# Queries and keys of the last batch: block-wise loads and a VectorE block transpose instead of TensorE transposes

## The chip, the core and the metric

The kernel runs on one core of a Trainium2 chip. The metric is the device time of one execution in microseconds (us). The core has five engines that run their own instruction queues in order and meet through semaphores: TensorE (PE; its weight loads are listed apart as PEld), VectorE (DVE), ScalarE (ACT), GpSimd (POOL) and SyncE (SP, which issues nearly all DMAs here).

## What is computed

Three layers follow one another: attention in which 32 global tokens see everything and 512 local tokens see the global ones and a window of 32 to either side; a two-layer perceptron over all tokens; and a soft mixture of experts. All data are float32, the two perceptron weights come as float64. Batch is 4, heads 8, head size 64. Cut to what matters:

```python
def _attn_ref(q_l, k_l, v_l, q_g, k_g, v_g):
    scale = 1.0 / np.sqrt(D)                      # D = 64
    def sm(s):
        s = s - np.max(s, axis=-1, keepdims=True)
        e = np.exp(s)
        return e / (np.sum(e, axis=-1, keepdims=True) + 1e-09)
    s_g = scale * np.matmul(q_g, k_all.transpose(0, 1, 3, 2))
    out_g = np.matmul(sm(s_g), v_all)
    s_ll = scale * np.matmul(q_l, k_l.transpose(0, 1, 3, 2))
    s_ll = np.where(np.abs(pos[:, None] - pos[None, :]) <= 32, s_ll, -1000000000.0)
    s_lg = scale * np.matmul(q_l, k_g.transpose(0, 1, 3, 2))
    a_l = sm(np.concatenate([s_lg, s_ll], axis=-1))
    out_l = np.matmul(a_l, np.concatenate([v_g, v_l], axis=2))
    return np.concatenate([out_g, out_l], axis=2)

def _moe_ref(x, w_in, w_out):
    h = x @ w_in
    return np.maximum(0.01 * h, h) @ w_out

def _moe2_ref(x, phi, w1, w2):
    logits = x @ phi                              # 32 slots, 8 experts
    slot_input = softmax_over_tokens(logits).T @ x
    slot_out = relu(slot_input[e] @ w1[e]) @ w2[e]   # for each expert e
    return softmax_over_slots(logits) @ slot_out
```

## The kernel before

**Pairs of heads.** Attention is done for 16 pairs (batch b, two heads i), counted here n = 4b + i; pairs 12 to 15 are those of batch 3. One pair goes through these steps:

- `load_qk` (L157): keys `kn` and queries `qn` come from memory with the token on the partition, two DMAs of 128 KB per tensor, in runs of 256 bytes (one token of one head). Both tiles have two buffers.
- `a_T` (L383): four 128x128 transposes on PE per tensor (L390) into a PSUM bank of the tag "tp" (two banks), and an ACT copy (L394) to `kT` (four buffers) and `qT` (two); the queries are multiplied by the scale in that copy. DVE then lays out the windows `kw` (L405 the keys of the window, L406 the global keys; three buffers, two per pair).
- `a_S` (L418): 32 small score matmuls (L434) into two banks of the tag "sc" (two banks), one for each head; DVE adds the mask and takes the maximum (L446), negates it (L452, `nmx`), ACT takes the exponential (L454).
- `a_E` (L465): eight transposes of the exponentials (L473) and two DVE copies (L477, `eT`); `a_V` (L481): 32 matmuls with the values (L493) and the division by the sum (L501, `xn`).

Each L434 or L493 instruction of the program shows as two matmul records in the trace.

After a batch's four `a_T`, `g_S` (L508) does the scores of its global tokens: matmuls `gl` (L519) over all four `kT` of the batch, again in the two "sc" banks, maxima on DVE (L530 to L532, `gnmx`), exponentials on ACT (L536, L542). A `kT` buffer is free for the next batch when these matmuls are done, an "sc" bank when its exponential is.

**Beside it runs the perceptron** of earlier tokens: `b_H` (L674), 12 matmuls of 128x512 per quarter (L689) into one of two "hb" banks, which ACT empties (L696, `g`); DVE block transposes `g` (L708) into `gb`, POOL moves the blocks (L717); then the soft router: `lg` (L740, L755, L800), DVE and ACT softmax (L759 to L795, ACT L764, L769, L792), and `up` (L810), which takes an "hb" bank too and is added up by DVE (L815).

**What sets the order.** Items of both strands are merged by weights written in the code (`step`, `b_items`, `merge`), and the framework then orders each engine's queue by a timeline of its own. What an engine does next is therefore fixed in the program: an instruction whose data are late holds all that stand behind it on that engine. `last_a` names the newest attention matmul, after which a held perceptron item may be issued.

**Loads** for pair n+2 are issued on SP when `a_T` of pair n is written, values (`load_v`, L167) when `a_V` is; SP waits in its queue until the buffer is free. `load_vn` (L203) brings the values of a whole batch, 1 MB in one DMA.

Of the kernel before, what the change touches and what calls it, by code (L numbers as in the profile page):

```python
# [8 lines left out]
F32 = mybir.dt.float32  # L9
# [11 lines left out]
def kernel(  # L21
# [15 lines left out]
    nc = tc.nc  # L37
    B, H, S, D = q_l.shape
# [23 lines left out]
    def tp(name):  # L62
        return bank("tp", name, 2)
# [93 lines left out]
    def load_qk(b, i, ts=(None, None)):  # L157
        for src, nm, t in ((k_l, "kn", ts[0]), (q_l, "qn", ts[1])):
            if t is None:
                t = sa.tile([P, NT, 2, D], F32, tag=nm, name=nm, bufs=2)  # L160
            for h in range(2):
                nc.sync.dma_start(
                    out=t[:, :, h, :], in_=src[b, 2 * i + h].rearrange("(t p) d -> p t d", p=P)
                )
            nat[nm, b, i] = t
# [217 lines left out]
    def a_T(b, i):  # L383
        qn, kn = nat.pop(("qn", b, i)), nat.pop(("kn", b, i))
        for src, dst, nm, bf in ((kn, kT, "kT", 4), (qn, qT, "qT", 2)):
            pt = tp(nm + "p")
            if b == 0:
                warm(pt)
            for T in range(NT):
                last_a[0] = nc.tensor.transpose(  # L390
                    pt[:, P * T:P * T + P], src[:, T].rearrange("p h d -> p (h d)"), ident
                ).ins
            t = sa.tile([P, S], F32, tag=nm, name=nm, bufs=bf)
            nc.scalar.activation(  # L394
                out=t, in_=pt, func=AF.Copy, scale=scale if nm == "qT" else 1.0,
            )
            dst[b, i] = t
        kt = kT[b, i]
        HW = NW // 2
        kwin[b, i] = []  # L400
        for hf in range(2):
            kw = sa.tile([P, HW, P], F32, tag="kw", name="kw", bufs=3)
            src = kt[:, 32 * HW * hf:32 * HW * hf + 96]
            src = bass.AP(src.tensor, src.offset, [src.ap[0], [32, HW], [1, 96]])
            nc.vector.tensor_copy(kw[:, :, 0:96], src)  # L405
            nc.vector.tensor_copy(  # L406
                kw[:, :, 96:128],
                kgT[:, i, 32 * b:32 * b + 32].unsqueeze(1).to_broadcast([P, HW, 32]),
            )
            kwin[b, i].append(kw)  # L410
# [7 lines left out]
    def a_S(b, i):  # L418
# [3 lines left out]
        sm = sa.tile([P, NT, 2], F32, tag="sm", name="sm", bufs=2)  # L422
        rs = sa.tile([P, NT, 2], F32, tag="rs", name="rs", bufs=2)
        es = []
        bks = [bank("sc", f"sc{e}", 2) for e in range(2)]
        if b == 0:
            for bk in bks:
# [12 lines left out]
        for e in range(2):  # L440
            bk = bks[e]
            s = sa.tile([P, S + SG], F32, tag="se", name="se", bufs=4)[:, 0:S].rearrange(
                "p (t k) -> p t k", t=NT
            )
            for T in range(NT):
                nc.vector.tensor_tensor_reduce(  # L446
                    out=s[:, T, :], in0=bk[:, P * T:P * T + P],
                    in1=mask[:, 0 if T == 0 else 2 if T == NT - 1 else 1, :],
                    scale=1.0, scalar=-3.0e38, op0=ALU.add, op1=ALU.max,
                    accum_out=mx[:, e, T:T + 1],  # L450
                )
            nc.vector.tensor_scalar_mul(nmx[:, e], mx[:, e], -1.0)  # L452
            for T in range(NT):
                exp_last[0] = nc.scalar.activation(  # L454
                    out=s[:, T, :], in_=s[:, T, :], func=AF.Exp,
                    bias=nmx[:, e, T:T + 1], accum_out=sm[:, T, e:e + 1],
                ).ins
            es.append(s)
        nc.vector.tensor_scalar_add(sm, sm, 1e-9)
# [921 lines left out]
```

## Time and profile before

| | |
|---|---|
| median of 3 runs | 500.24 us (499.12 to 501.63) |
| profiled execution, its own time | 496.2 us |
| span of the profile | 494.5 us |
| PE busy | 463.5 us, 94% of the span |
| DVE, ACT, POOL busy | 56%, 47%, 32% |
| granted PE clock, mean | 0.979 of full speed |

All times of single instructions below come from the one profiled execution, whose span is 494.5 us. They are counted from the start of that span. Matmuls overlap, so what a group of them costs is read from its first start to the first start of the next group; the duration written beside it is longer. Batch 3 goes through attention between about 190 us (first load) and 325 us.

### The profile page before, as it was taken

The numbers are of one execution on the slowest core, as the hardware profiler recorded it, in microseconds if no ns is written. First come the engines' busy times: TensorE is split into PE (matmuls) and PEld (weight loads), VectorE is DVE, ScalarE is ACT, GpSimd is POOL, SyncE is SP. The second block draws the span as 40 slices with busy tenths as digits, with TensorE's granted clock in tenths as the row PEclk, the third lists the DMA queues.
The fourth block names the chain that finished last, engine by engine and source line by source line (L and its number), as shares of the span: only waits on it lengthen the run. The fifth ranks groups of instructions, "written<-read, shape, count | busy, mean of one in ns | idle before, by whom it ended". The sixth has DMA issues, their size and how long they took to land.

```text
span 494.5 us, 13438 instructions
## 1 busy us (share of the span) xinstructions
PE 463.5 (94%) x5323; PEld 322.0 (65%) x5323; DVE 275.0 (56%) x886; ACT 234.3 (47%) x680; POOL 160.3 (32%) x281
## 2 busy tenths in 40 slices
PE   7867889999989999999999999999999999999993
PEld 5645668666766657776777676777777777533463
DVE  4585888498547776556554656427666511413332
ACT  4776899588655345543435444234444432201122
POOL 2044887342400113460615243243667700000000
PEclk9986899999999999999999999999999999999998
DMA  9989598599457655334250231169420079999977
GB/s 177 223 200 267 183 292 313 185 304 311 150 143 144 143 118 93 85 76 129 60 106 1 60 60 45 44 220 405 150 78 2 23 266 357 364 397 371 305 237 214
DMA packets 118362, 90.23 MB, mean 182 GB/s; under 512 B 75356, under 2 KB 100764, under 8 KB 118300
## 3 DMA queue, kind: packets, MB, share of 16 engines
q1 hardware_dynamic: 115628, 88.33, 61.8%
q10 hardware_dynamic: 2672, 1.05, 0.8%
q8 instruction: 42, 0.69, 0.6%
q14 instruction: 20, 0.16, 0.1%
HBM read 76.68 MB, written 8.65 MB: 173 GB/s over the span
## 4 chain that ended last, share of the span: by engine, by line
PE 78%; DVE 4%; ACT 4%; DMA 1%; issue 1%; POOL 0%; ACTq 0%; DVEq 0%; POOLq 0%
PE hp L689 38%; PE gtp L726 4%; PE ehp L1221 3%; PE sc L434 3%; PE up L810 3%; PE po L493 3%; PE lg L740 2%; PE etp L473 2%; PE sop L1297 2%; PE sop L1275 1%; PE gpo L579 1%; PE wotp L345 1%; PE qTp L390 1%; PE kTp L390 1%; PE xtp L659 1%; PE gl L519 1%
## 5 line engine op out<-in xcount | busy, mean ns | idle before, releaser
L689 PE MATMUL hp<-wi,xxh 128*128 128x512 f32 x512 | 167.2, 408 | 1.2 <-ACT xxh L665 1.2
L689 PEld LDWEIGHTS hp<-wi,xxh 128*128 128x128 f32 x512 | 91.8, 190 | 28.2 <-issue 8.2
L717 POOL COPY g<-gb 32x256 f32<-32x256 f32 x206 | 82.7, 401 | 82.6 <-DVE gb L708 55.5
L689 PE MATMUL hp<-wi,xxl 128*128 128x512 f32 x256 | 101.0, 396 | 0.0
L696 ACT ACTIVATE g<-hp 128x512 f32<-128x512 f32 x60 | 35.3, 595 | 56.2 <-PE hp L689 54.2
L454 ACT ACTIVATE se<-se,nmx 128x128 f32<-128x128 f32 x128 | 49.6, 390 | 21.5 <-DVE nmx L452 21.4
L689 PEld LDWEIGHTS hp<-wi,xxl 128*128 128x128 f32 x256 | 48.3, 189 | 12.5 <-issue 1.7
L200 POOL COPY vw<-vw 32x1664 f32<-32x1664 f32 x10 | 15.8, 1575 | 78.3 <-DMA vw<-in_v_g_dram 34.9
L446 DVE CUSTOM_DVE_ANT_0 se<-sc,mask 128x128 f32<-128x128 f32 x128 | 28.9, 284 | 12.1 <-PE sc L434 12.0
L261 POOL TENSOR_TENSOR wn<-wn,rraw 128x512 int32<-128x512 int32 x16 | 22.8, 1435 | 34.5 <-DVE wn L257 33.0
L708 DVE STREAM_TRANSPOSE gb<-g 128x512 f32<-128x512 f32 x32 | 22.2, 702 | 19.3 <-ACT g L696 14.0
L434 PE MATMUL sc<-kw,qT 64*32 64x128 f32 x1024 | 29.2, 283 | 0.8 <-DVE mx L446 0.4
L493 PE MATMUL po<-vw,eT 128*32 128x64 f32 x1024 | 24.2, 232 | 3.5 <-issue 2.1
L261 POOL TENSOR_TENSOR wo<-wo,rraw 128x512 int32<-128x512 int32 x12 | 16.0, 1332 | 31.7 <-DVE wo L257 7.2
L434 PEld LDWEIGHTS sc<-kw,qT 64*32 64x32 f32 x1024 | 19.8, 109 | 8.9 <-issue 5.3
L493 PEld LDWEIGHTS po<-vw,eT 128*32 128x32 f32 x1024 | 18.4, 116 | 10.2 <-issue 7.4
L477 DVE COPY eT<-etp 128x512 f32<-128x512 f32 x28 | 18.7, 684 | 9.9 <-PE etp L473 9.9
L454 ACT ACTIVATION_READ_ACCUMULATOR se<-se,nmx 128x1 f32 x128 | 24.1, 188 | 0.0
L473 PE MATMUL etp<-identr,se 128*128 128x128 f32 x128 | 22.4, 296 | 0.2
L405 DVE COPY kw<-kT 128x672 f32<-128x672 f32 x32 | 19.8, 653 | 3.1 <-ACT kT L394 2.7
L251 ACT ACTIVATE rraw<-rraw 128x512 int32<-128x512 uint32 x28 | 18.7, 673 | 4.3 <-DMA rraw<-in_moe_w_out_dram 3.1
L473 PEld LDWEIGHTS etp<-identr,se 128*128 128x128 f32 x128 | 15.8, 146 | 6.3 <-ACT se L454 2.3
(232 smaller groups left out, 777.9 us busy)
## 6 DMA issues: line engine op xcount, KB each, us to landing
ew<-in_moe_w_dram SPq DMA_DIRECT2D x23, 1024.0 KB, 9.5
rraw<-in_moe_w_in_dram SPq DMA_DIRECT2D x16, 512.0 KB, 5.5
vw<-in_v_l_dram SPq DMA_DIRECT2D x60, 112.0 KB, 3.2
rraw<-in_moe_w_out_dram SPq DMA_DIRECT2D x12, 512.0 KB, 6.7
ew<-in_moe_w_dram SPq DMA_DIRECT2D x9, 512.0 KB, 9.2
ew<-in_moe_w_dram SPq DMA_DIRECT2D x17, 256.0 KB, 5.5
wo_f<-wo SPq DMA_DIRECT2D x16, 256.0 KB, 3.2
vn<-in_v_l_dram SPq DMA_DIRECT2D x4, 1024.0 KB, 6.3
```

The costliest lines, as they stand in the source:

```text
L261: nc.gpsimd.tensor_tensor(out=di, in0=di, in1=m, op=ALU.add)
L405: nc.vector.tensor_copy(kw[:, :, 0:96], src)
L434: last_a[0] = nc.tensor.matmul(bks[e][32 * u:32 * u + 32, P * T:P * T + P], qt[64 * e:64 * e + 64, 32 * U:32 * U + 32], kw[win(U) // (NW / ...
L446: nc.vector.tensor_tensor_reduce(out=s[:, T, :], in0=bk[:, P * T:P * T + P], in1=mask[:, 0 if T == 0 else 2 if T == NT - 1 else 1, :], sca ...
L454: exp_last[0] = nc.scalar.activation(out=s[:, T, :], in_=s[:, T, :], func=AF.Exp, bias=nmx[:, e, T:T + 1], accum_out=sm[:, T, e:e + 1],).ins
L473: last_a[0] = nc.tensor.transpose(pt[:, P * T:P * T + P], es[e][:, T, :], ident).ins
L493: last_a[0] = nc.tensor.matmul(pov[32 * u:32 * u + 32, T, e, :], ets[e][:, 32 * U:32 * U + 32], vw[:, win(U), e, :], start=True, stop=True ...
L689: nc.tensor.matmul(hp, a[:, k, :], w[c][:, k, :], start=(k == 0 and n == 0), stop=(k == KD - 1 and n == 2),)
L696: nc.scalar.activation(out=gs, in_=hp, func=AF.Prelu, alpha=0.01)
L708: nc.vector.transpose(out=gb[:, f % 2], in_=gs)
L717: copy(dst[32 * c:32 * c + 32, :, a], src[32 * a:32 * a + 32, :, c])
L726: nc.tensor.transpose(pt[:, P * c:P * c + P], g[:, o:o + P], ident)
```

## The change

For batch 3 alone (`b >= 3`): keys and queries are loaded by four DMAs of 64 KB per tensor in runs of 128 bytes, so that partition 64h + 32c + k holds, for token k of each window of 32, half c of head h. One VectorE transpose of 32x32 blocks per tensor then gives `kT` or `qT` as they were. The eight PE transposes, the two "tp" banks and the two ACT copies of a pair go. The scale of the queries, which sat in the ACT copy, goes into the negated maximum and into the exponential (a constant in an instruction that is there anyway). Over four pairs: 32 PE transposes and 8 ACT copies less, 8 DVE block transposes more, 32 load DMAs where there were 16.

```diff
@@ load_qk
             if t is None:
                 t = sa.tile([P, NT, 2, D], F32, tag=nm, name=nm, bufs=2)
+            if b >= 3:
+                t = t.rearrange("p t h d -> p (t h d)").rearrange("p (w d) -> p w d", d=32)
             for h in range(2):
+                if b >= 3:
+                    for c in range(2):
+                        g = 64 * h + 32 * c
+                        nc.sync.dma_start(
+                            out=t[g:g + 32],
+                            in_=src[b, 2 * i + h, :, 32 * c:32 * c + 32].rearrange(
+                                "(w k) d -> k w d", k=32
+                            ),
+                        )
+                    continue
@@ a_T
         for src, dst, nm, bf in ((kn, kT, "kT", 4), (qn, qT, "qT", 2)):
+            if b >= 3:
+                t = sa.tile([P, S], F32, tag=nm, name=nm, bufs=bf)
+                nc.vector.transpose(out=t, in_=src.rearrange("p w d -> p (w d)"))
+                dst[b, i] = t
+                continue
@@ a_S
+        sc_q = scale if b >= 3 else 1.0
...
-            nc.vector.tensor_scalar_mul(nmx[:, e], mx[:, e], -1.0)
+            nc.vector.tensor_scalar_mul(nmx[:, e], mx[:, e], -sc_q)
...
-                    bias=nmx[:, e, T:T + 1], accum_out=sm[:, T, e:e + 1],
+                    bias=nmx[:, e, T:T + 1], scale=sc_q, accum_out=sm[:, T, e:e + 1],
```

The change also moves instructions, since the framework orders the queues anew. The order is the same on every engine up to where pair 10 is worked on; it differs from there to where pair 15 is done, and in a few places behind that. In the rows of the changed kernel the line numbers are higher by 17 or 18 (L434 is L452, L689 is L707, L530 is L548); L400 is the new block transpose, L167 the new load.

DVE, from the maxima of the global scores of batch 2 on. Before:

```order
L530 TENSOR_REDUCE gmx<-gl 128x1 x2
L759 TENSOR_REDUCE nm<-lg 128x1
L763 TENSOR_TENSOR nm<-nm 128x1
L531 TENSOR_REDUCE gmx<-gg 128x1
L768 TENSOR_TENSOR al<-nm 128x1
L531 TENSOR_REDUCE gmx<-gg 128x1
L532 TENSOR_REDUCE gnmx<-gmx 128x1 x2
```

And in the changed kernel, up to the second `gnmx`:

```order
L548 TENSOR_REDUCE gmx<-gl 128x1
L400 STREAM_TRANSPOSE kT<-kn 128x512 x2
L548 TENSOR_REDUCE gmx<-gl 128x1
L777 TENSOR_REDUCE nm<-lg 128x1
L422 COPY kw<-kT 128x7x96 x2
L423 COPY kw<-kgT 128x7x32 x2
L549 TENSOR_REDUCE gmx<-gg 128x1 x2
L422 COPY kw<-kT 128x7x96
L781 TENSOR_TENSOR nm<-nm 128x1
L550 TENSOR_REDUCE gnmx<-gmx 128x1
L519 TENSOR_TENSOR xn<-po,rs 128x4x128
L550 TENSOR_REDUCE gnmx<-gmx 128x1
```

The key transposes of pairs 12 and 13, the windows of pair 12 and the first one of pair 13 have moved in between the first maximum of the global scores and `gnmx`; the key transpose of pair 14 is the next row, that of pair 15 stands 22 rows and the query transposes of pairs 14 and 15 stand 33 and 81 rows further on.

PE, from the end of a perceptron quarter to the next one, around `a_V` of pair 10. Before:

```order
L689 MATMUL hp<-wi,xxl 128x512
L493 MATMUL po<-vw,eT 32x64 x17
L800 MATMUL lg<-identr,st 128x128
L493 MATMUL po<-vw,eT 32x64 x14
L390 MATMUL kTp<-identr,kn 128x128 x4
L493 MATMUL po<-vw,eT 32x64
L810 MATMUL up<-g,d 32x512 x4
L390 MATMUL qTp<-identr,qn 128x128 x4
L689 MATMUL hp<-wi,xxh 128x512 x2
```

And now:

```order
L707 MATMUL hp<-wi,xxl 128x512
L511 MATMUL po<-vw,eT 32x64 x32
L452 MATMUL sc_3649<-kw,qT 32x128 x16
L491 MATMUL etp<-identr,se 128x128 x4
L818 MATMUL lg<-identr,st 128x128
L452 MATMUL sc_3650<-kw,qT 32x128 x10
L491 MATMUL etp<-identr,se 128x128 x4
L452 MATMUL sc_3650<-kw,qT 32x128 x6
L511 MATMUL po<-vw,eT 32x64 x2
L744 MATMUL gtp<-identr,g 128x128 x4
L828 MATMUL up<-g,d 32x512 x4
```

The scores of pair 12 (sc_3649 for the first head, sc_3650 for the second, in the two banks that `gl` of batch 2 leaves) have moved up to directly behind `a_V` of pair 10, where before the first of them stood four, the last twelve groups of the perceptron later.

ACT, from a `gT` copy or `g` to the next evictions, around the exponentials of pair 13. Before:

```order
L728 COPY gT<-gtp 128x512 x2
L454 ACTIVATE se,sm<-se,nmx 128x128 x4
L696 ACTIVATE g<-hp 128x512
L454 ACTIVATE se,sm<-se,nmx 128x128 x4
L665 ACTIVATE xxh<-xtp 128x512
```

And now:

```order
L714 ACTIVATE g<-hp 128x512
L472 ACTIVATE se,sm<-se,nmx 128x128 x5
L746 COPY gT<-gtp 128x512 x2
L472 ACTIVATE se,sm<-se,nmx 128x128 x3
L714 ACTIVATE g<-hp 128x512 x2
L683 ACTIVATE xxh<-xtp 128x512
```

The eviction that stood between the two sets of exponentials now stands behind both, with two copies among them.

On SP the loads of pairs 12 and 13 keep their places; the queries of pairs 14 and 15 are now issued next, eight DMAs, then six of the eight for the keys, the 1 MB `vn` of batch 2, and the last two. Before, `vn` stood between the keys and the queries of pair 14.

## Rows read from the trace of the kernel before

**Rows 1.** Windows: stretch, length, each engine's busy time (records), PEclk, DMA share, GB/s.
```profile
225.00:250.00 25.00, 25.00 (x375) 18.41 (x374) 15.04 (x55) 10.70 (x37) 7.92 (x17) 1.00 0.46 110
250.00:275.00 25.00, 25.00 (x330) 17.46 (x329) 12.62 (x56) 10.08 (x34) 7.90 (x17) 1.00 0.27 54
```
**Rows 2.** Windows, PE alone: eight groups of L390 (batch 3), each to the next group.
```profile
225.63:226.22 0.59, 0.59 (x9) 1.00 0.10 28
...
285.43:285.84 0.41, 0.41 (x11) 1.00 0.00 0
sum 3.97, PE 3.97; mean PE 0.50
```
**Rows 3.** Timeline of PE: start, length, operation; `a_V` of pairs 10 and 11.
```profile
224.12 0.75 PE L493 MATMUL po<-vw,eT 128*32 128x64 f32 x34
...
235.19 1.10 PE L493 MATMUL po<-vw,eT 128*32 128x64 f32 x64
```
**Rows 4.** Timeline of PE: scores in one piece, and a piece of 14.
```profile
200.57 1.16 PE L434 MATMUL sc<-kw,qT 64*32 64x128 f32 x64
201.66 0.50 PE L689 MATMUL hp<-wi,xxh 128*128 128x512 f32 x1
...
234.82 0.44 PE L434 MATMUL sc<-kw,qT 64*32 64x128 f32 x14
```
**Rows 5.** Timeline of DVE (idle before and releaser in brackets): maxima of the global scores.
```profile
222.00 1.29 DVE L530 TENSOR_REDUCE gmx<-gl 128x1 f32<-128x512 f32 x2 [1.25 <-PE gl L519]
223.20 0.28 DVE L759 TENSOR_REDUCE nm<-lg 128x1 f32<-128x128 f32 x1
...
223.89 0.27 DVE L532 TENSOR_REDUCE gnmx<-gmx 128x1 f32<-128x2 f32 x2
```
**Rows 6.** Timeline of DVE: a block transpose and the windows of pair 11.
```profile
207.63 0.71 DVE L708 STREAM_TRANSPOSE gb<-g 128x512 f32<-128x512 f32 x1 [0.17 <-ACT g L696]
208.26 0.98 DVE L405 COPY kw<-kT 128x672 f32<-128x672 f32 x2
209.16 0.47 DVE L406 COPY kw<-kgT 128x224 f32<-128x224 f32 x2
```
**Rows 7.** Timeline of ACT: from the router's exponential to the first global one.
```profile
223.77 0.37 ACT L764 ACTIVATE st<-lg,nm 128x128 f32<-128x128 f32 x1 [3.12 <-DVE gmx L531]
...
224.22 0.68 ACT L536 ACTIVATE gs<-gl,gnmx 128x512 f32<-128x512 f32 x1
```
**Rows 8.** Groups by line, 224 to 312 us: count, busy us, mean ns, idle before.
```profile
L454 ACT ACTIVATE se<-se,nmx 128x128 f32<-128x128 f32 x32 | 12.4, 390 | 7.3 <-DVE nmx L452 7.3
...
L446 DVE CUSTOM_DVE_ANT_0 se<-sc,mask 128x128 f32<-128x128 f32 x32 | 7.1, 282 | 4.4 <-PE sc L434 4.4
...
L728 ACT COPY gT<-gtp 128x512 f32<-128x512 f32 x7 | 3.8, 586 | 1.4 <-PE gtp L726 1.4
...
L815 DVE SCALAR_TENSOR_TENSOR uacc<-uacc,al,up 128x512 f32<-128x512 f32 x4 | 3.0, 743 | 0.8 <-PE up L810 0.8
```
**Rows 9.** Timeline of PE: from `up` over a perceptron quarter and four transposes to scores.
```profile
252.17 1.07 PE L810 MATMUL up<-g,d 128*32 128x512 f32 x8
...
256.56 0.43 PE L434 MATMUL sc<-kw,qT 64*32 64x128 f32 x10
```
**Rows 10.** DMA issues by tile: count, KB each, us to landing; below, from SP's timeline.
```profile
phis<-in_moe_phi_dram SPq DMA_DIRECT2D x1, 64.0 KB, 2.7
...
qn<-in_q_l_dram SPq DMA_DIRECT2D x2, 128.0 KB, 5.8
...
226.32 0.94 SPq L162 DMA_DIRECT2D kn<-in_k_l_dram  x2
```
**Rows 11.** Two windows early in the kernel, and PE's longest idle time at full clock.
```profile
44.00:48.00 4.00, 3.62 (x67) 2.95 (x67) 1.53 (x4) 0.80 (x2) 1.27 (x1) 0.50 1.06 284
62.00:100.00 38.00, 36.16 (x216) 26.56 (x220) 26.18 (x47) 30.19 (x67) 23.41 (x20) 1.00 0.78 265
...
63.66 0.73 PE L689 MATMUL hp<-wi,xqn 128*128 128x512 f32 x2 [1.92 <-ACT xqn L665]
```

## The prediction

> **What bounds the kernel now.** I read the windows first, over the stretch in which batch 3 goes through attention [rows 1]: PE is busy for the whole of both windows, 50 of 50 us, at full granted clock, while DVE, ACT and POOL have 40% to 68% of the time free and the DMA engines are busy for 0.27 to 0.46. So PE's queue sets the pace here, no other engine and no transfer, and work taken off PE shortens the kernel by what it costs there, as long as nothing new makes PE wait. Work added to DVE costs nothing unless PE waits for DVE. PE runs its queue in order, so I then walked the new order of the queues, with durations from the trace before, and looked for the first instruction on PE whose data come late.
>
> **What is removed from PE.** Eight groups of four transposes. The windows that reach from each group's first start to the next group's first start add up to 3.97 us [rows 2]. All of it lies on the path, since PE has no idle time there: -4.0 us. The bounds are narrow, since this is the time of the very instructions that go. (Each of these matmuls is drawn 0.27 us long, but the next starts 0.10 us behind it.) The Trainium skill, in "TensorE: Matmul & The Clock Gate", Part 4, gives about 275 ns for a 128x128 transpose in a kernel. By that figure, taken for all 32, the removal would be worth 8.8 us, and the rows speak against it, because four of them with their change-over end within 0.41 to 0.59 us. The eight ACT copies are worth nothing on the path: ACT is busy for 10.1 to 10.7 of 25 us [rows 1]. The scale in the exponential is a constant in an instruction that is issued anyway: nothing.
>
> **What the new order does to PE's own work.** Counting pieces (runs of one line on PE) from the first moved row to the end, the old order has 230, of which 8 are the transposes; the new one has 234. So there are 12 more cuts: scores 10 to 15 pieces, transposes of exponentials 6 to 10, global scores 3 to 6, one more of another kind, and one less of `a_V`. A cut is not free. 64 score records in one piece take 1.09 us to the next start, 14 take 0.37 (234.82 to 235.19) [rows 3, 4]; that is 0.0144 us for a record and 0.17 for a piece. 12 x 0.17 = +2.0 us. The lower bound is half of that, where a piece ends in front of a kind that starts without a gap (a transposing group that is followed by the perceptron takes 0.41, four times 0.10 and no more [rows 2]); the upper bound is 2.4.
>
> **What is added to DVE, and where it lands.** Eight block transposes of 128x512; L708 has the same form, one starts 0.63 us before the next instruction [rows 6]. That is 5.0 us on an engine that is busy for 12.6 to 15.0 of 25 us [rows 1]. What matters is the queue position. The query transposes of pairs 12 and 13 stand where DVE has idle time or is ahead of its readers: nothing. The key transposes of pairs 12 and 13 stand between the two maxima of the global scores of batch 2. Behind them on DVE wait the second maximum, the router's `nm` and `gnmx`; for `gnmx` waits the ACT exponential that empties the first "sc" bank; and for that bank waits PE, because the scores of pair 12 now come directly behind `a_V` of pair 10.
>
> The working: the first maximum starts at 222.00, as before, since nothing ahead of it is delayed. Then 0.60 for it, 2 x 0.63 for the transposes, 0.60 for the second maximum, 0.31 for `nm` [rows 5], 0.90 and 0.40 for the windows of pair 12 [rows 6], 0.30 for two small maxima, 0.45 for the first window of pair 13, 0.16 and 0.15 for `nm` and the first `gnmx`: 5.1 us, so `gnmx` is there at 227.1, where it was at 224.0 [rows 5]. ACT does the router's exponential first (0.45 to the next) and then the global one, 0.68 long [rows 7]: 227.0 + 0.45 + 0.68 = 228.1. PE is through with `a_V` of pair 10 at 224.12 + 1.03 = 225.2 (64 records, first start to the next; drawn 1.10) [rows 3]. PE waits **2.9 us**, with nothing else to do, where it had no wait at all. Bounds: 2.3 if DVE's small instructions overlap better than I add them, 3.5 if the transposes take their full 0.71.
>
> I followed the three queues from there to the end of pair 13. The next thing late is the eviction of a perceptron bank, which now stands behind all exponentials of pair 13. When PE has the last scores of pair 13, it needs about 4.4 us to the next scores (`up`, a quarter, four transposes [rows 9]) and 3.6 for a few scores and the next quarter: 8.0, then it wants that bank. DVE meanwhile takes eight maxima (0.21 apart; 0.28 long), a query transpose, a window and the sum of `up` (0.74) [rows 8]: 3.8; then ACT eight exponentials of 0.39, two copies of 0.59 [rows 8] and the eviction, about 4.8. 8.6 against 8.0: **0.6 us**, between 0 and 1.5.
>
> **The loads.** 32 of 64 KB for 16 of 128 KB. A load with the same run and size is in the trace: `phis`, landed after 2.7 us. SP needs 0.47 us for an issue [rows 10], so a pair takes it 3.8 us instead of 1.9, of some 20 that a pair lasts; the values, which are queued behind, start up to 2 us later and have some 10 to spare. The tight ones are the keys of pairs 14 and 15. Those of pair 14 wait for the buffer of pair 12, free at 223.3; the fourth is issued at 224.7 and lands at 227.4, DVE comes to the transpose at 227.9: no wait. The last two of pair 15 are issued behind `vn`; queries behind `vn` landed after 5.8 us [rows 10], which gives 232.9, about when DVE gets there. I take 0 for it, and price the other case below. The Trainium skill says in "DMA: Bandwidth & Descriptors", Specifications, that transfers reach line rate only from 512 bytes on, which speaks against cutting runs from 256 to 128. The landing of `phis` does not show a loss for so small a transfer, and by the DMA share [rows 1] rate is not what is short; the rule leaves the sum as it is, unless the loads come late, which is rival B.
>
> **The sum.** -3.97 + 2.0 + 2.9 + 0.6 = +1.5 us, on the profiled execution's 496.2 us: 497.7. That execution lies 4.0 us under the median of the runs, 500.24, and I carry the difference along: **501.8 us**, +0.3%. What comes behind pair 15 has nearly the old order and starts 1.5 us later.
>
> **The rivals.** 0.5% (2.5 us) is about what a measurement can tell from no change, so "faster" begins under 497.7 and "slower" over 502.7.
>
> A: PE does not wait for the "sc" bank, because ACT has emptied it by then. For it: PE stands still nowhere in this stretch before [rows 1]. Against: the three queues are in order, and I see no way around the two transposes. -3.97 + 2.0 + 0.6 = -1.4: 498.9; with cuts at half price and no late eviction 497.3, which is faster.
>
> The transposes cost PE more than the windows say, 0.27 us each: 32 x 0.27 = 8.7 instead of 3.97, and the time is 497.1. For it: each is drawn 0.27 long. Against: the starts [rows 2]. The Trainium skill's figure above would come out so.
>
> B, on the other side: DVE stops for a load. The key transposes of pairs 14 and 15 wait in DVE's queue, and the copies of the exponentials, the router's softmax and the sum of `up`, which frees a perceptron bank for PE, stand behind them. There are 0.5 us to spare for pair 14 and none for pair 15. It decides from a landing of 3.2 us on for pair 14 or 6 for pair 15. If the keys of pair 14 take 5.8 [rows 10], DVE stands for 2.6 us and PE soon after it: 504.3.
>
> C, also slower: PE's clock drops after the wait. PE's longest idle time amid full work was 1.92 us and the granted clock stayed at 1.00, 2.4 GHz, in the window around it [rows 11]; one of 2.9 is not in the trace. Early in the kernel, where PE stops again and again, the granted clock is 0.50 in a window of 4 us with PE busy for 3.62 of it [rows 11]. Four such microseconds behind the wait would cost 2.0: 503.8.
>
> **How the numbers follow.** Forecast 0.56; A 0.11; dearer transposes 0.04; B 0.16; C 0.13. Faster by over 0.5%: the dearer transposes and four hundredths of A, 0.08. Slower: B, C and four hundredths of the forecast (wait and eviction at their upper bounds give +3.0), 0.33. Within: 0.59. For eight in ten the range goes from 498.3 (A with no late eviction) to 504.8 (B with a little of the forecast's upper side): below it lie 0.08, above it about a third of B and C, 0.10.
>
> **What would show it.** Right: no L390 work for pairs 12 to 15; eight more block transposes of 0.7 us; PE idle for 2 to 3.5 us ahead of the scores of pair 12, released by the global exponential on ACT, near 225 us; PE otherwise without idle time but for tenths; more, shorter pieces. Wrong: no idle time there (A); 32 transposes missed by 8 us of PE (dearer); idle DVE ahead of a block transpose, released by a DMA (B); a granted clock under 1.00 behind 225 us (C).

## The result and the profile after

The changed kernel takes 506.07 us (median; 501.13 to 508.52) against 498.47 (497.23 to 501.63) for the kernel before, timed beside it on the same chips: a ratio of 1.0137, 95% interval 1.0107 to 1.0167. It is slower by 7.6 us, and the prediction (501.8, range 498.3 to 504.8) was too low. Medians, here and below, leave out two executions in a slower state of the chip, one of e2_fill and one of e10_loads.

The profiled execution of after took 504.86 us, its span is 503.1:

```profile
span 503.1 us, 13398 instructions
PE 467.3 (93%) x5291; PEld 322.6 (64%) x5291; DVE 277.9 (55%) x894; ACT 229.7 (46%) x672; POOL 159.6 (32%) x281
```

PE is busy for 467.3 us, 3.8 more than before, with 32 transposes less to do. Busy time that grows while work is taken away is the first thing to notice. The windows of after, in the columns of [rows 1], say where:

```profile
225.00:250.00 25.00, 22.32 (x279) 14.87 (x282) 16.42 (x61) 8.31 (x34) 2.50 (x7) 0.86 0.38 84
250.00:275.00 25.00, 25.00 (x327) 17.93 (x320) 10.92 (x46) 9.23 (x31) 11.58 (x24) 1.00 0.21 41
230.00:238.00 8.00, 8.00 (x82) 4.29 (x70) 5.82 (x33) 1.59 (x10) 0.00 (x0) 0.58 0.60 153
```

Where PE was busy for 25 of 25 us at full clock [rows 1], it now stands still for 2.68 us, and in the 8 us behind that it is busy all the time at a granted clock of 0.58 on the mean. All idle time of PE of more than 0.1 us between 195 and 335 us, from its waits (total, times, longest):

```profile
PE sc L452 <- ACT gs L554: 2.7, 1, 2.7
PE gxt L610 <- DVE xg L605: 0.4, 1, 0.4
```

PE's timeline around the stop (start, length, operation, idle before and releaser), which answers to [rows 3]:

```profile
225.71 1.10 PE L511 MATMUL po<-vw,eT 128*32 128x64 f32 x64
229.49 1.08 PE L452 MATMUL sc<-kw,qT 64*32 64x128 f32 x32 [2.68 <-ACT gs L554]
230.50 0.66 PE L491 MATMUL etp<-identr,se 128*128 128x128 f32 x4
230.99 0.27 PE L818 MATMUL lg<-identr,st 128*128 128x128 f32 x1
231.19 1.43 PE L452 MATMUL sc<-kw,qT 64*32 64x128 f32 x20
232.56 1.11 PE L491 MATMUL etp<-identr,se 128*128 128x128 f32 x4
...
236.00 1.94 PE L828 MATMUL up<-g,d 128*32 128x512 f32 x8
237.87 0.83 PE L707 MATMUL hp<-wi,xxh 128*128 128x512 f32 x2
```

Four transposes of exponentials take 0.66 us at 230.50 and 1.11 at 232.56; `up` takes 1.94 where it took 1.07 [rows 9]. This is the lower clock: 0.50, so 1.2 GHz, from about 231.3 to 238.1.

DVE's timeline, which answers to [rows 5, 6], and ACT's, to [rows 7]:

```profile
223.58 0.69 DVE L548 TENSOR_REDUCE gmx<-gl 128x1 f32<-128x512 f32 x1 [0.80 <-PE gl L537]
224.19 1.29 DVE L400 STREAM_TRANSPOSE kT<-kn 128x512 f32<-128x512 f32 x2
225.41 0.65 DVE L548 TENSOR_REDUCE gmx<-gl 128x1 f32<-128x512 f32 x1
...
228.20 0.15 DVE L550 TENSOR_REDUCE gnmx<-gmx 128x1 f32<-128x2 f32 x1
...
229.54 0.71 DVE L400 STREAM_TRANSPOSE kT<-kn 128x512 f32<-128x512 f32 x1 [0.54 <-DMA kn<-in_k_l_dram]
...
236.39 0.71 DVE L400 STREAM_TRANSPOSE kT<-kn 128x512 f32<-128x512 f32 x1 [1.99 <-DMA kn<-in_k_l_dram]
```
```profile
228.31 0.37 ACT L782 ACTIVATE st<-lg,nm 128x128 f32<-128x128 f32 x1 [1.90 <-DVE nm L781]
228.67 0.68 ACT L554 ACTIVATE gs<-gl,gnmx 128x512 f32<-128x512 f32 x1
```

From the start of the first maximum to the end of the first `gnmx` it is 4.77 us (5.1 predicted), then two exponentials on ACT, the router's and the global one, then PE. DVE does wait for keys, 0.54 and 1.99 us, and PE never through it. A load of 64 KB of keys lands after 2.3 us (median):

```profile
kn<-in_k_l_dram SPq DMA_DIRECT2D x16, 64.0 KB, 2.3
```

**The ledger.** I compare one stage, from PE's first `gl` of batch 2 to the first `a_V` matmul of pair 15: 220.87 to 310.58 before, 222.45 to 318.35 after. That is +6.19 us; behind it come +0.47 (the `gxt` wait) and +0.42 at the end. The stage begins between 220.6 and 224.9 in the profiled executions of all these kernels, because the granted clock of the early part differs from execution to execution; so I compare stage lengths, and medians beside them. Each line's time is taken from start to next start:

| in the stage | us | from |
|---|---|---|
| transposes of keys and queries gone | -3.96 | kTp -2.14, qTp -1.82 |
| PE's stop | +2.68 | the wait above |
| lower clock | +2.94 | same work in e2_fill: 3.74, here 6.68 |
| scores of one head standing together | +1.24 | 53 neighbours x 0.0233, from e4_heads |
| other order of PE's work | +3.29 | the rest |
| sum | +6.19 | |

The line before the sum is what remains, and no edit prices it by itself. e2_fill below has the same order at full clock; there the scores take 2.63 us more than before, the global scores (`gl`, `gg`) 0.97, the transposes of exponentials 0.64 and two other transposes (`gtp`, `xtp`) 0.50.

The ledger is that of one execution. Of the others the record has the granted clock, as a mean over the whole span: 0.967 on the mean of the 15 executions of after, 0.974 to 0.975 in the four sets of the kernel before, 86 executions, that were timed beside the experiments. 6.8 us at 0.50 lower such a mean by 0.007. The two shortest times of after, 501.13 and 501.95, have the two highest clocks, 0.974 and 0.981. So the lower clock is in most executions of after, and perhaps not in these two.

### The profile page after: what moved, and what is told of

It is laid out like the page before. It is cut to its first block, busy times and chain, and to the rows that moved or that the text cites. A ratio compares the mean times of both kernels' runs of the same rounds, so it can differ in the third digit from the quotient of the medians.

```text
span 503.1 us, 13398 instructions
## 1 busy us (share of the span) xinstructions
PE 467.3 (93%) x5291; PEld 322.6 (64%) x5291; DVE 277.9 (55%) x894; ACT 229.7 (46%) x672; POOL 159.6 (32%) x281
## 4 chain that ended last, share of the span: by engine, by line
PE 75%; DVE 5%; ACT 3%; DMA 3%; issue 1%; POOL 0%; ACTq 0%; SPq 0%; DVEq 0%; POOLq 0%
PE hp L707 37%; PE sc L452 4%; PE up L828 4%; PE gtp L744 4%; PE ehp L1239 3%; PE lg L758 3%; PE etp L491 2%; PE po L511 2%; PE sop L1315 2%; PE sop L1293 1%; PE xtp L677 1%; PE op L1339 1%; DMA rraw<-in_moe_w_out_dram 1%; PE wm L85 1%; DMA rraw<-in_moe_w_in_dram 1%
## 5 line engine op out<-in xcount | busy, mean ns | idle before, releaser
L707 PE MATMUL hp<-wi,xxh 128*128 128x512 f32 x512 | 167.1, 408 | 1.2 <-ACT xxh L683 1.2
L707 PEld LDWEIGHTS hp<-wi,xxh 128*128 128x128 f32 x512 | 92.0, 190 | 29.1 <-issue 10.1
L707 PE MATMUL hp<-wi,xxl 128*128 128x512 f32 x256 | 101.4, 397 | 0.0
L707 PEld LDWEIGHTS hp<-wi,xxl 128*128 128x128 f32 x256 | 48.3, 189 | 13.5 <-issue 1.7
L452 PE MATMUL sc<-kw,qT 64*32 64x128 f32 x1024 | 33.2, 288 | 3.9 <-ACT gs L554 2.7
L452 PEld LDWEIGHTS sc<-kw,qT 64*32 64x32 f32 x1024 | 22.1, 110 | 12.5 <-issue 5.3
L491 PE MATMUL etp<-identr,se 128*128 128x128 f32 x128 | 23.9, 302 | 0.3
```

Source lines behind the costliest of these rows:

```text
L452: last_a[0] = nc.tensor.matmul(bks[e][32 * u:32 * u + 32, P * T:P * T + P], qt[64 * e:64 * e + 64, 32 * U:32 * U + 32], kw[win(U) // (NW / ...
L491: last_a[0] = nc.tensor.transpose(pt[:, P * T:P * T + P], es[e][:, T, :], ident).ins
L707: nc.tensor.matmul(hp, a[:, k, :], w[c][:, k, :], start=(k == 0 and n == 0), stop=(k == KD - 1 and n == 2),)
```

## The experiments

In most of them the queues are fixed, so that an edit moves nothing but itself. At the end of the kernel each instruction of one engine gets an edge to the one that shall stand ahead of it in that engine's queue; the edge is no wait.

```python
for a, b in zip(order, order[1:]):        # places in program order
    tc.add_manual_dep(q[b], q[a].name, DependencyInfo(NoSync, DATA), reason="issue_after")
```

"Fixed to before" means that the tables hold the order of the kernel before. DVE, ACT, POOL and SP are fixed with PE unless the text says otherwise. "Stage" gives the length against before's 89.71 us.

### Is it the order? PE back in the old order

```diff
+ORDERS = {"PE": <order of before, less the 32 transposes>}    # on the changed kernel; the other engines free
```

> The changed kernel, with PE's queue held in the order of the kernel before (less the 32 transposes); the other queues are ordered anew. Theory O (the new order costs it all: a wait of 2.7 us, 3.4 us more behind it at half clock, and some 4 us for scores of one head in a row and for shorter pieces): all three go, the removal stays, 4.0 us under the kernel before, about 494.5, ratio 0.992; no idle time ahead of the scores of pair 12 and no granted clock under 1.00 there. Rival D (the block transposes on DVE or the loads in short runs cost it): still at or over the kernel before, 498 or more. Rival E (each transpose is worth its 0.27 us): 489.8, ratio 0.983.

502.06 against 498.06 us, 1.0082 (1.0055 to 1.0110); stage +3.75. The theory that the old order on PE is enough falls. The stop moved to the next reader behind the key transposes in DVE's queue, and grew (PE, then DVE):

```profile
229.71 0.47 PE L855 MATMUL lg<-identr,st 128*128 128x128 f32 x1 [4.47 <-DVE st L820]
```
```profile
222.98 1.29 DVE L437 STREAM_TRANSPOSE kT<-kn 128x512 f32<-128x512 f32 x2
...
228.58 0.71 DVE L437 STREAM_TRANSPOSE kT<-kn 128x512 f32<-128x512 f32 x1 [1.39 <-DMA kn<-in_k_l_dram]
229.22 0.12 DVE L823 TENSOR_TENSOR al<-nm 128x1 f32<-128x1 f32 x1
229.37 0.28 DVE L820 COPY st<-lg 32x128 f32<-32x128 f32 x1
```

The router's `lg` waits for `st`, a copy that stands behind three key transposes, the third held by a load for 1.39 us. That is the mechanism of rival B, in another order than the changed kernel's. The granted clock fell to 0.50 for 6.8 us here too, from 227.25 to 234.1: the last 2.5 us of the stop and 4.4 us of work behind it.

### What does the lower clock cost? The stop filled with matmuls

```diff
         po = bank("po", "po", 1)
+        if (b, i) == (2, 2):
+            for _ in range(12):
+                warm(po)          # 128x512, overwritten by a_V; queues fixed to the changed kernel
```

> The changed kernel with every queue held in its own order, and 12 matmuls of 128x512 that nobody reads put in ahead of a_V of pair 10 (0.217 us from one start to the next, 2.6 us), so that PE works through the time in which it stood still. Theory C (the clock falls because PE stood still): the 2.7 us stay spent, now as work, but the granted clock stays at 1.00 behind 231 us and the 3.4 us that half clock cost there come back: about 502.7, ratio to the kernel before 1.0085. Rival (the clock falls for another cause in that stretch, or the wait is for something that moves along): half clock stays, 506 or more, ratio 1.015.

502.81 against 498.06, 1.0102 (1.0069 to 1.0135); stage +3.59, 2.85 of it the filling and 0.25 a wait for the router's `st` that the changed kernel doesn't have. The order is that of the changed kernel, and the clock stays up:

```profile
231.00:238.00 7.00, 7.00 (x74) 4.22 (x75) 5.73 (x28) 2.51 (x11) 0.00 (x0) 1.00 0.38 99
```
```profile
229.78 0.85 PE L519 MATMUL sc<-kw,qT 64*32 64x128 f32 x20
...
233.52 0.73 PE L777 MATMUL hp<-wi,xxh 128*128 128x512 f32 x2
```

From the 20 scores to the next quarter it is 3.74 us; the same work takes 6.68 in the changed kernel (231.19 to 237.87). So the lower clock costs 2.94 us. By these traces the stop and the clock together are 5.6 us. The medians agree, and less sharply: with 2.85 us of filling in place of 2.68 of stop the ratio is 1.0102 where it was 1.0137, 1.7 us less, and the two intervals overlap. The mean granted clock of the five executions is 0.975, that of the kernel before.

### Does a stop bring the lower clock down with nothing else changed? Three stops

```diff
+    zt_ = sa.tile([P, 2, P], F32R, name="zt_", bufs=1)
@@ a_V, pair 10; the kernel before, fixed
+        if (b, i) == (2, 2):
+            for n in range(2):
+                nc.tensor.matmul(po[:, 0:P], identr, zt_[:, 0, :], start=True, stop=True)
+                for _ in range(6 * (1 - n)):        # e7_short_stop: 3
+                    nc.gpsimd.tensor_copy(zt_[0:32], mask[0:32, 0:2, :])
```

> The kernel before with every queue held in its own order, and nothing changed but that PE is made to stand still ahead of a_V of pair 10: it reads a small tile, GpSimd (which has nothing else to do there) writes that tile six times, and PE reads it again; some 2.4 to 3 us. Theory C (a stop at full load takes the clock with it): the stop and 3.4 us more at half clock behind it, 6.1 us in all, about 504.6, ratio 1.012. Rival (a stop costs itself alone): 2.7 us, 501.2, ratio 1.0055, granted clock 1.00.

504.53 against 498.06, 1.0130 (1.0101 to 1.0159): as expected. PE stood for 2.78 us, and behind it:

```profile
227.02 0.33 PE L554 MATMUL po<-zt__150,identr 128*128 128x128 f32 x1 [2.78 <-POOL zt__150 L556]
```
```profile
228.00:231.60 3.60, 3.60 (x44) 2.03 (x43) 1.55 (x8) 0.98 (x3) 0.00 (x0) 0.53 0.04 11
```

A stop alone, in the old order with all transposes on PE, can take the clock down, here for 3.4 us (about 1.7 us lost; stage +5.67). 0.92 of the stage is a second wait further on, which is taken up below.

> As e3, with three writes by GpSimd in place of six: PE stands still for about 1.5 us ahead of a_V of pair 10, and nothing else is changed. If the clock goes with any stop at full load: 1.5 us and 1.7 us more at half clock, 3.2 us, about 501.3, ratio 1.0065. If only a longer stop takes it (the 1.92 us of the kernel before, at 63.66 us, left it at 1.00): 1.5 us, 499.6, ratio 1.003, granted clock 1.00 behind it.

501.66 against 497.29, 1.0085 (1.0055 to 1.0116). Stop 1.43 us, granted clock 1.00 throughout; stage +2.84, of which 0.97 is the second wait. The expectation with a falling clock was near the time but not for its reason. e12_port, further on, has the same stop, 1.42 us, and there the clock did fall. One row of each (e7_short_stop, then e12_port):

```profile
229.00:230.00 1.00, 1.00 (x10) 0.24 (x3) 0.98 (x3) 0.38 (x1) 0.00 (x0) 1.00 0.08 19
```
```profile
229.00:230.00 1.00, 1.00 (x29) 0.83 (x26) 0.63 (x5) 0.38 (x2) 0.00 (x0) 0.50 0.00 0
```

So the length of a stop doesn't decide it alone. Behind stops of 2.7 to 4.5 us in the stage the clock fell in all four traces that have one; behind 1.4 it fell in one of two, behind 0.86 (e9_hold_keys) it did not. The stop of 1.92 us [rows 11] has a counterpart in every trace, far ahead of the stage: near 62 us PE waits for `xqn`, for 1.29 to 2.54 us, each time from full clock. In six of the fourteen traces the clock then went to 0.50 for 3.4 us (stops of 1.67, 1.71, 1.88, 2.08, 2.29 and 2.52 us), in eight it stayed (1.29, 1.31, 1.42, 1.71, 1.72, 1.92, 1.97 and 2.54). The shortest stop of the six (e5_places) and the longest of the eight (e4_heads):

```profile
64.18 0.73 PE L769 MATMUL hp<-wi,xqn 128*128 128x512 f32 x2 [1.67 <-ACT xqn L745]
```
```profile
65.20:68.60 3.40, 3.40 (x9) 2.64 (x8) 2.61 (x5) 2.96 (x6) 3.37 (x3) 0.50 0.95 299
```
```profile
64.29 0.73 PE L757 MATMUL hp<-wi,xqn 128*128 128x512 f32 x2 [2.54 <-ACT xqn L733]
```
```profile
64.30:68.60 4.30, 4.30 (x18) 3.26 (x19) 3.30 (x5) 3.12 (x7) 4.12 (x4) 1.00 0.94 289
```

What else decides it, no run here shows.

### What do scores cost when a head stands alone?

```diff
+ORDERS = {"PE": <before; in pairs 12 to 15 the scores of head 0 ahead of those of head 1, in the same places>}
```

> The kernel before with every queue held in its own order, but in pairs 12 to 15 the scores of the first head stand ahead of all scores of the second, where before the heads took turns; the pieces are as many and as long. Theory H (two scores of one head in a row take twice the time of two that take turns, 0.055 against 0.027 us for an instruction): 115 such neighbours x 0.027 = 3.1 us, about 501.6, ratio 1.006. Rival (the order within a piece makes no difference, as the prediction took it): no change, 498.5, ratio 1.000.

500.36 against 498.06, 1.0063 (1.0042 to 1.0084); stage +3.23, of which the scores are +2.68 and 0.52 is the second wait. The piece of 32 records in the kernel before, and here:

```profile
241.07 0.67 PE L434 MATMUL sc<-kw,qT 64*32 64x128 f32 x32
```
```profile
241.97 1.08 PE L502 MATMUL sc<-kw,qT 64*32 64x128 f32 x32
```

The heads' keys lie in the lower and the upper 64 partitions. Inside such a piece, instructions that alternate between them start 0.027 us apart on the mean, those of one half 0.055. The Trainium skill says in "TensorE: Matmul & The Clock Gate", Part 3, that a weight load overlaps with matmuls in flight only when its row group of the array is another; these starts agree with it. Over the whole stage the 115 neighbours cost 2.68 us, 0.0233 for one, a little less than the 3.1 expected. In the changed kernel 53 score instructions stand behind one of their own half that did not before: 53 x 0.0233 = 1.24 us.

### What is a piece worth?

```diff
+ORDERS = {"PE": <before; in two places hp x6, etp x8 becomes hp, etp, hp, etp, ...>}
```

> The kernel before with its queues fixed, except that in two places of the stretch (ahead of the copies of the exponentials of pairs 13 and 15) six perceptron matmuls and the eight transposes of exponentials behind them, which stand as two pieces on PE, alternate one by one: 20 more pieces, and not one instruction more or less. The step of the prediction (0.17 us for a piece) expects +3.4 us in the stretch, 501.7 us, a ratio of 1.007. The price that the trace of the changed kernel suggests for the cuts of the same transposes (0.22 us for a piece, clock left out) expects +4.4, 502.7, 1.009. If a transposing group is nothing dearer when it alternates with the perceptron (the lower bound of the step, half), +1.7, 500.0, 1.0035. In all cases the granted clock stays at 1.00 and PE has no idle time but for tenths.

498.6 against 498.47, 1.0010 (0.9983 to 1.0037); stage +0.09. Twenty more pieces cost nothing: all three prices were wrong for this kind. Both kinds use the whole array (128*128):

```profile
265.05 0.50 PE L755 MATMUL hp<-wi,xxh 128*128 128x512 f32 x1
265.39 0.27 PE L539 MATMUL etp<-identr,se 128*128 128x128 f32 x1
265.42 0.48 PE L755 MATMUL hp<-wi,xxh 128*128 128x512 f32 x1
```

The perceptron matmul that follows starts 0.03 us behind the transpose, which gives back what its own start lost. With that in mind I sorted all changes of line in the stage of before by the tile they use. From 128*128 to a narrow tile (64*32, 128*32) the next start comes 0.08 us late, back from 128*32 0.135, back from 64*32 0.185: 0.22 to 0.27 for a visit. A piece of this kind has no price; a change of tile has one by these starts, which no edit tested. The stage of after has 85 changes of tile, that of e5_places (the order of before without the transposes) 71. The 14 more, at 0.08 to 0.19 each, make 1.1 to 2.7 of the 3.29 us in the ledger's rest.

### The block transposes held behind `gnmx`

```diff
@@ a_T, on the changed kernel; all else free
+                with tc.issue_after(g_last[0]):          # gnmx of the last batch
                     nc.vector.transpose(out=t, in_=src.rearrange("p w d -> p (w d)"))
```

> The changed kernel with one edge more: the block transposes of a pair stand on DVE behind the last negated maximum of the global scores before them (for pairs 12 to 15: batch 2); the framework orders the rest anew. Read along the new queues: the maxima and gnmx come as early as before, so the sc banks are free in time; but both transposes of pairs 12 and 13 stand together ahead of the windows of pair 12, and PE now wants the scores of pair 12 directly behind a_V of pair 10 and the exponentials' transposes: by the durations before, PE is there 2.6 us behind a_V's start and the windows are done 4.2 us behind it. So PE waits about 1.7 us for DVE's windows of pair 12, under the 1.9 us that left the clock alone. Pieces on PE: 13 more than are left without the transposes, at 0.2 us, 2.6; 22 scores behind one of the same head, 0.6. Theory (the queue decides, and a stop this short leaves the clock): -4.0 + 1.7 + 2.6 + 0.6 = +0.9 us, 498.2, ratio 1.002, granted clock 1.00 to the end of pair 15. Rival (the clock falls too): +3.5 more, 501.5, ratio 1.009. Rival (the wait was the keys' place alone, and goes with it): -4.0, 493.5.

499.71 against 498.09, 1.0029 (1.0005 to 1.0052); stage +1.70. PE waits once in the stage, 0.86 us, for the windows of pair 12 and no longer for the exponential; granted clock 1.00 from 218 to 313:

```profile
PE sc L454 <- DVE kw L424: 0.9, 1, 0.9
```

One edge on each of the eight transposes, with the queues made anew around it, takes back 4.5 of the stage's 6.19 us. What stays is the order of PE's work: -3.96 + 0.86 leaves +4.8 to the stage's 1.70. That is near the 4.5 of the ledger (1.24 + 3.29), though the order is another one, with 22 such neighbours of one head (by the expectation) in place of 53. The time came within 1.5 us of the expected 498.2 partly by luck: the wait was half of the 1.7 expected, and the order cost 4.8 in place of 3.2.

### The change for the queries alone

```diff
-            if b >= 3:
+            if b >= 3 and nm == "qn":      # in a_T: nm == "qT"; all queues free
```

> The change for the queries alone: keys are loaded and turned on PE as before, queries by DVE; the queues are ordered anew by the framework. 16 PE transposes go, worth 1.82 us by their first starts. Theory Q (the key transposes ahead of the maxima of the global scores do the damage): no wait on PE of over half a microsecond between 220 and 320 us, no granted clock under 1.00 there, and the new order has no score of one head behind another of the same head: 1.8 us under the kernel before, 496.3, ratio 0.996. Rival D (any block transpose or short-run load there costs it): at or over the kernel before.

503.66 against 497.29, 1.0123 (1.0092 to 1.0155); stage +4.99. Not faster, so it isn't enough to leave the key transposes where they were. The order was made anew here too, and PE stops at another place, for 3.06 us, for a copy that stands behind eight exponentials and an eviction on ACT:

```profile
PE etp L491 <- ACT gT L746: 3.1, 1, 3.1
```
```profile
282.13 0.40 ACT L472 ACTIVATE se<-se,nmx 128x128 f32<-128x128 f32 x1 [2.60 <-DVE nmx L470]
...
285.22 0.57 ACT L714 ACTIVATE g<-hp 128x512 f32<-128x512 f32 x1
285.70 1.05 ACT L746 COPY gT<-gtp 128x512 f32<-128x512 f32 x2
```

The clock was at 0.50 for 6.8 us, from 0.5 us ahead of the stop's end. This is the kind of wait that the prediction saw behind pair 13 ("late eviction"), at a place and size of its own.

### The gain without a new order

```diff
@@ a_T, on the kernel before, fixed
+            if b >= 3:
+                nc.scalar.activation(out=t, in_=src.rearrange("p t h d -> p (t h d)"), func=AF.Copy, scale=...)
+                continue
```

> The kernel before with every queue held in its own order, less the 32 PE transposes of batch 3 and nothing else: ACT copies keys and queries from the loaded tiles as they are, so what batch 3 computes is not the attention. It prices the first term alone. By the first starts in the trace before: -3.97 us, 494.1, ratio 0.992. If each transpose is worth its 0.27 us: -8.7 us, 489.4, ratio 0.9825. If PE's time there is covered by something else: no change.

495.39 against 497.29, 0.9961 (0.9945 to 0.9978). Stage -3.45: kTp and qTp -3.96, and small waits of 0.3 and 0.2 back. The step of 3.97 us stands; the dearer transposes (-8.7) don't.

```diff
+ORDERS = {"PE": <before, less the transposes>, "DVE": <before, 8 block transposes where DVE was idle>,
+          "Activation": <before, less the copies>, "Pool": <before>}    # on the changed kernel
```

> The changed kernel, with the queues of PE, DVE, ACT and GpSimd held in the order of the kernel before (less the 32 transposes and their 8 copies), and the eight block transposes put where DVE stood idle in the trace before: keys of pair 12 right ahead of its windows, its queries ahead of the copies of the exponentials of pair 11, pair 13 ahead of the copies of the transposed global exponentials of batch 2, pair 14 ahead of the maxima of pair 13, pair 15 behind the negated maxima of pair 14. Theory Q (the time is lost by where the key transposes stand in DVE's queue, ahead of what PE waits for; e1 still had them there and stopped for 4.5 us): nothing on PE waits, the clock stays, and the removal is left: 4.0 us under the kernel before, 494.1, ratio 0.992. Rival D (transposes on DVE or loads in short runs cost it wherever they stand): no better than the kernel before, 498 or more. Rival E (a PE transpose is worth its 0.27 us): 489.4.

495.51 (493.25 to 497.82) against 497.29, **0.9965 (0.9944 to 0.9986)**; stage -3.30. This computes everything, and beats both kernels. The rest of PE's idle time, and the window that had the stop:

```profile
PE sc L514 <- DVE qT L462: 0.4, 1, 0.4
PE lg L880 <- DVE st L845: 0.2, 1, 0.2
PE hp L769 <- ACT g L776: 0.2, 1, 0.2
```
```profile
225.00:250.00 25.00, 24.45 (x376) 16.83 (x371) 17.03 (x58) 8.27 (x32) 8.80 (x20) 1.00 0.56 112
```

The medians of both show half of what the stage shows, 1.8 and 1.9 us; their profiled stages began 4.0 and 2.8 us later than before's, in a part that the edits don't touch. I can't say whether that belongs to the kernels or to those executions.

### The loads alone, and the second wait

```diff
@@ load_qk, on the kernel before; PE, DVE, ACT, POOL fixed, SP free: the new loop of the change, nothing else
```

> The kernel before with the queues of PE, DVE, ACT and GpSimd held in their own order, and keys and queries of batch 3 loaded as in the change, 32 times 64 KB in runs of 128 bytes; they are turned on PE as before, so the blocks stand elsewhere and what batch 3 computes is not the attention. It prices the loads alone. As predicted: nothing waits for them, no change, 497.3, ratio 1.000. Rival B (short runs land late): PE stops ahead of a transpose of pair 14 or 15, released by a DMA, by 1 us or more.

499.28 against 498.09, 1.0017 (0.9989 to 1.0046): no difference. No wait of PE is released by a load. Stage +1.11, of which 1.02 is the second wait that e3_stop, e4_heads, e7_short_stop and e12_port have, 0.5 to 1.0 us long:

```profile
PE qTp L462 <- ACT kT L466: 1.0, 1, 1.0
```

ACT's copy stands behind eight exponentials, and these started late, because DVE's negated maximum, a 128x4 instruction of 0.15 us, took ten times as long. Beside it POOL's copy in the values' window:

```profile
246.51 1.47 DVE L524 TENSOR_SCALAR nmx<-mx 128x4 f32<-128x4 f32 x1
```
```profile
246.38 1.57 POOL L272 COPY vw<-vw 32x1664 f32<-32x1664 f32 x1
```

The maximum ends at 247.98, the copy at 247.95. In all ten traces where they meet near 245 us (before among them) the held maximum ends 0.02 to 0.03 us behind the copy. In before the first of the two maxima started 0.17 us ahead of the copy, and only the second was held, 0.91 us long, without a wait on PE. The seven of these traces that have before's order with its transposes divide by this: where the first maximum is held (e10_loads and the four named above), PE has the second wait, and where the second is held (before, e11_cuts), it has not. The Trainium skill says in "SBUF — State Buffer", Who interferes with whom, that VectorE and GpSimd share a port pair, and that an instruction which takes it holds it to its end while the other engine's blocks; the trace agrees, 1.47 us for 0.15.

> The kernel of the short stop (e7_short_stop) with one instruction moved on POOL: the copy of 32x1664 in the values' window, 1.58 us long, stands four block copies earlier. In e7_short_stop DVE's negated maximum (128x4, 0.15 us long elsewhere) took 1.41 us, from 245.99 to 247.40, and POOL's copy ran from 245.80 to 247.38; in the kernel before the same maximum started 0.17 us ahead of that copy and took 0.15. Theory: DVE is held by the POOL copy, ACT's eight exponentials start late by that, and PE's second wait (0.97 us for the key copy on ACT) comes from it; moved, the maximum takes 0.15 to 0.5, the second wait is under 0.3, the stretch +1.9 instead of +2.84, and the time 499.2 (ratio 1.0045 instead of 1.0085). Rival: the second wait comes of the stop itself, because PE's queue stands later against ACT's: the wait stays at 0.9 to 1.0, the time at 501 (1.0085).

```diff
 ORDERS["Pool"]: on e7_short_stop
-    g<-gb x16, vw<-vw
+    g<-gb x12, vw<-vw, g<-gb x4
```

500.92 against 498.47, 1.0048 (1.0023 to 1.0072), but the edit didn't do what it should: POOL then waited in front of the copy for 1.84 us, and it met the maximum again.

```profile
248.52 1.39 DVE L519 TENSOR_SCALAR nmx<-mx 128x4 f32<-128x4 f32 x1
```
```profile
248.31 1.57 POOL L267 COPY vw<-vw 32x1664 f32<-32x1664 f32 x1 [1.84 <-PE geg L637]
```

The second wait stayed (1.0). That the maximum is held by the copy is seen in ten traces; that the wait goes with it is seen in how these traces divide, and no edit showed it. Its stage, +4.27, has the lower clock of one execution in it, and the median doesn't reach that far. By the record the clock didn't fall in every execution: its mean over the twelve executions is 0.9742, that of the kernel before beside them 0.9745, and 3.4 us at 0.50 in each would make 0.003. For the result the second wait has no part: the changed kernel doesn't have it.

## Why the prediction was wrong

Step by step, by its own terms:

- **Removal, -3.97.** Right: -3.96 in after and in e6_removed.
- **The wait, +2.9 (2.3 to 3.5).** Right in place, releaser and size: 2.68 us ahead of the scores of pair 12, released by the global exponential. DVE's part was 0.4 us shorter than added up, since its small instructions start closer behind one another than the sum took them. Rival A (no wait) is out.
- **The clock.** This is the first of two steps that failed: the prediction had the mechanism as rival C, gave it 0.13 and left it out of the forecast, on the ground that a stop of 1.92 us [rows 11] left the clock at 1.00. That row said nothing of 2.7, and it was one outcome of several: the same stop took the clock down in six of the fourteen traces. e2_fill and e3_stop show from both sides that the stop brought it. It was also mis-sized: 2.0 us guessed as four microseconds at half rate, 2.94 measured, 6.8 us at 0.50.
- **Cuts, 12 x 0.17 = +2.0 (1.0 to 2.4).** The second step that failed, in kind and in size. e11_cuts shows that pieces of one tile size cost nothing, while by the starts in before's trace a change of tile costs 0.22 to 0.27 there and back. Worse, the price was taken from a piece of 64 records in which the heads alternate [rows 3, 4], and the new order, shown ahead of the prediction, has 16 scores of one head in a row: +1.24 us, with no term at all. Together with what else the order changed it is +4.5 in place of 2.0, and of the 3.29 in it that are the ledger's rest the cause is open in part.
- **Late eviction behind pair 13, +0.6.** It didn't show: PE's waits in after hold none for an eviction, and the perceptron's own time in the stage grew by 0.04. The term was within its bounds (0 to 1.5).
- **Loads, 0.** Right for PE. DVE waited 0.54 and 1.99 us for keys, which is B's mechanism, and PE's work behind it was not late; e1_old_order shows what happens when it is.

So +1.5 became +6.19: 2.94 for the clock, 1.24 for the heads and 1.29 for the rest of the order came on top, 0.6 of the eviction and 0.2 of the wait did not come. Either failed step alone would have left the prediction's sum inside its range (504.7 with the clock, 504.3 with the order); together they put it outside. With all these sizes the sum gives 501.8 + 2.94 + 1.24 + 1.29 - 0.6 - 0.2 = 506.5, and that 506.07 was measured is luck in part: the sum starts from 500.24, the median of three executions, and beside the changed kernel the one before took 498.47. From there the stage's 6.19 and the 0.89 behind it give 505.6.

## What to carry to other kernels

An edit that takes work off a saturated engine is worth its time only in the order that it was priced in: price the new order, and if the gain is real, fix the old order and place the new instructions by hand (here +1.4% became -0.35%). Where the bounding engine stood never idle, a new stop costs itself and what the clock does behind it; price both together. One row of a stop without a drop doesn't license leaving the clock out: the same stop, of 1.3 to 2.5 us, took it down in six of fourteen traces. Price a cut by the tile on either side and by the half of the array that its neighbours use, not by the number of pieces.

## What was not expected of the hardware

- Behind a stop of 2.68 us amid full work PE ran at 1.2 GHz for 6.8 us, behind 2.78 for 3.4, behind 3.06 for 6.3 and behind 4.47 for 4.4. Behind one of 1.42 it did in one trace and in another, with 1.43, it did not; behind the stop near 62 us it did after 1.67 and did not after 2.54.
- Inside a piece, 64-row matmuls that alternate between the halves start 0.027 us apart on the mean, those of one half 0.055.
- Alternating a 128x512 matmul with a 128x128 transpose is free (20 more pieces, +0.09 us); a visit to a narrow tile costs 0.22 to 0.27 us by the starts in before's trace.
- A DVE instruction of 0.15 us took up to 1.47 beside a POOL copy, and ended 0.02 to 0.03 us behind it in ten traces.
